# A constant product moved behind each turn of transposes, and the last weights loaded in blocks of 8, 3, 1, 1, 1

## The chip, the cores and the metric

The kernel runs on one core of a Trainium2 chip. The metric is the time of one execution on the device in microseconds (us): the median of three runs before the change. One further execution was profiled; all durations below come from it.

## The reference

One decoding step for a batch of two: attention of 32 query heads over the last 4096 positions of a cache with 8 key/value heads, and a small dense block with the Mish activation, mixed by a gate.

```python
W = min(4096, max(256, Sk // 4))                     # 4096 of 32768 positions
q = (x @ wq).reshape(B, Sq, Hq, Dh)                  # B 2, Sq 1, D 512, Hq 32, Dh 128
scores = jnp.einsum("bhqd,bhkd->bhqk", q, k) * (Dh ** -0.5)
o = jnp.einsum("bhqk,bhkd->bhqd", softmax(scores), v)
a = o.reshape(B, Sq, Hq * Dh) @ wo                   # 4096 x 512
h = jnp.einsum("bsd,df->bsf", x, w1) + b1            # 512 x 1792
b = jnp.einsum("bsf,fd->bsd", h * jnp.tanh(softplus(h)), w2)   # 1792 x 512
g = sigmoid((x * gate_w).sum(-1, keepdims=True))
return g * a + (1 - g) * b
```

Everything is float32. About 91 MB of weights and cache are read once.

## The kernel before

**Loads.** All large inputs are streamed by the sync engine's queue (SP) into two buffers of 4 MB, `buf_a` and `buf_b`, which take turns: wq in two halves, then for each of 8 key/value heads its keys into `buf_b` and its values into `buf_a`, then w1 into `buf_b`, wo in two halves (`buf_a`, then `buf_b`), and at last w2. A load waits until TensorE has finished the step that read the buffer before (L356 to L361). SP issues in the order of the program, so a load that waits holds back all that stand behind it.

**w2** is 14 blocks of 128 x 512 (256 KB each). `CUTS` (L35) gives the cuts into five loads. The first two loads go into `buf_a`, behind its first `PART` = 5 places, and wait for the step "A wo"; the other three are single blocks, go into a small tensor `rest` of their own, and wait for nothing but their turn on SP (L363 to L366).

**Steps of TensorE (PE).** A "B" step (`step_b`, L406) works through the 16 places ("slots") of `buf_b`, an "A" step (`step_a`, L417) through those of `buf_a`: one product of a 128 x 32 stationary operand with 128 x 512 for each slot. A float32 product shows as two records in the profile, so a step has 32. Slot s writes the 32-row strip s % 4 of its bank, and slots on different strips run side by side. A "T" step is a "turn" (L409): wait for the semaphore `st`, which says that another engine has written the tile `turn`; four transposes of it; and one small product with `ones` (L413) whose end is told on the semaphore `pe`, on which VectorE (DVE), ScalarE (ACT), GpSimd (POOL) and SP wait. The order of steps is the list at L128: B q0, T q0, A q1, B s0, T p0, T q1, A v0; then B s, T p, A v for each head 1 to 7 (for the last one with T mx between T p7 and A v7); then B h, T ms, T oa, T ob, T hs, A wo, B wo, A w2. PE runs this as a loop over three pieces of code: after a turn a bit of a register says whether another turn follows or an A step (L414 to L416).

**The constant product** is `idle_work` (L392): the identity matrix times itself repeated, 128 x 128 by 128 x 512, into a bank that nobody reads. It runs in the loop "spin" (five times after each A step, once after the tenth), and, before the change, once ahead of each A step.

**The last step** A w2 uses its first 5 slots with zero weights; slot `PART` waits for the first w2 load (semaphore `s4`), slot `PART + CUTS[1]` for the second (`s12`) (L419). VectorE then adds the bank to `sums` (L322). After that `finish` (L329) multiplies the three blocks in `rest` and `sums` into one bank, in the order block 11, block 12, sums, block 13; VectorE copies the result (L344), and SP stores it (L367).

Of the kernel before, what the change touches and what calls it, by code (L numbers as in the profile page):

```python
# [31 lines left out]
SMALL = DC * B + DC + FC  # L32
SCALE = DH ** -0.5
CAP = 20.0
CUTS = (0, 6, 11, 12, 13, 14)  # L35
ROWS = (24, 104)
WIDE = 2 * Q - B
PART = SLOTS - CUTS[2]
SPINS = 5
# [46 lines left out]
def decode_kernel(nc, res, stored, small, wq, k_in, v_in, w1, wo, w2, out):  # L86
    def sb(name, *shape, parts=P):
        n = 1
        for s in shape:
            n *= s  # L90
        t = nc.alloc_sbuf_tensor(name, [parts, n], F32).ap()
        if len(shape) == 1:
            return t
        names = "abcd"[: len(shape)]
        return t.rearrange(f"p ({' '.join(names)}) -> p {' '.join(names)}", **dict(zip(names[1:], shape[1:])))
# [5 lines left out]
    buf_b = sb("buf_b", CHUNK)  # L101
    rest = sb("rest", FC - CUTS[2], D)
    sm = sb("sm", SMALL)
    xT = sm[:, : DC * B].rearrange("p (c b) -> p c b", b=B)
    gw = sm[:, DC * B : DC * B + DC]
    b1 = sm[:, DC * B + DC :]
    sizes = (SLOTS * Q, SLOTS * Q, HKV * BH + B, HKV * BN * (Q + REP), (FC - CUTS[2]) * WIDE, WIDE)
    zeros = sb("zeros", sum(sizes))
# [8 lines left out]
    sa, sb_, st, s4, s12, sx = (nc.alloc_semaphore(n) for n in ("sa", "sb", "st", "s4", "s12", "sx"))  # L117
    sr = [nc.alloc_semaphore(f"sr{x}") for x in range(FC - CUTS[2])]
    pe = Lane(nc, nc.tensor, "pe")
# [180 lines left out]
    for i, (dst, sem) in enumerate(((la, sa), (lb, sb_))):  # L300
# [11 lines left out]
    t = pool.add(lambda: G.tensor_tensor(nu, nu, de, op=ALU.mult), t)  # L312
    act2_ok = pool.add(lambda: G.tensor_tensor(act2[:, :, Q - B : Q], nu[:, CUTS[2] :], ho[:, CUTS[2] :], op=ALU.mult),
                       t, ho_ok)
    sums = sb("sums", D)
    t = act.add(lambda: S.copy(sums, g_a), at("A wo"))
    pool.add(lambda: G.memset(la[:, : PART * Q], 0.0), t, sem=sa, by=got + 2)
    pool.add(lambda: G.tensor_tensor(la.rearrange("p (s q) -> p s q", q=Q)[:, PART:, ::RS], nu[:, : CUTS[2]],
                                     ho[:, : CUTS[2]], op=ALU.mult), sem=s4)
# [49 lines left out]
    def slots(bank, weights, buf, ready):  # L369
        for s in range(SLOTS):  # L370
            if s in ready:
                T.wait_ge(*ready[s]).then_inc(ready[s][0], -ready[s][1])  # L372
            ins = T.matmul(bank[Q * (s % NJ) : Q * (s % NJ) + Q, :], weights[:, s * Q : (s + 1) * Q],  # L373
                           buf[:, s * D : (s + 1) * D], start=(s < NJ), stop=(s >= SLOTS - NJ))
            if s == SLOTS - 1:
                ins.then_inc(pe.sem, 1)
# [5 lines left out]
    with nc.Block(no_gpsimd_drain=True) as block:  # L382
        @block.sync
        def _(eng):
            sp.emit(eng)

        @block.tensor
        def _(eng):
            base = nc.cur_bb
            n, again, bit, spin = (nc.alloc_register(eng.engine, x) for x in ("steps", "again", "bit", "spin"))  # L390

            def idle_work():  # L392
                T.matmul(b_idle, ident, ident[:, None, :].to_broadcast([P, NT, P]), start=True, stop=True)  # L393


            def part(name):
                nc.switch_body(name, parent=base, valid_engines=[eng.engine])

            eng.reg_mov(n, FULL - steps_a)
            eng.reg_mov(again, turns)  # L400
            eng.br("step_b")
            part("spin")
            idle_work()
            eng.reg_add(spin, spin, 1)
            eng.br_lt(spin, SPINS, "spin", "step_b")
            part("step_b")  # L406
            slots(g_b, lb, buf_b, {0: (sb_, got + 1)})
            eng.br_eq(n, FULL, "step_a", "turn")
            part("turn")  # L409
            T.wait_ge(st, 1).then_inc(st, -1)  # L410
            for c in range(NT):
                T.transpose(t_b[:, c * P : (c + 1) * P], turn[:, c * P : (c + 1) * P], ident)  # L412
            T.matmul(b_s[:, : HKV * BH + B], ones, kx, start=True, stop=True).then_inc(pe.sem, 1)  # L413
            eng.reg_alu(bit, again, 1, ALU.bitwise_and)  # L414
            eng.reg_alu(again, again, 1, ALU.logical_shift_right)
            eng.br_eq(bit, 1, "turn", "step_a")  # L416
            part("step_a")  # L417
            idle_work()
            slots(g_a, la, buf_a, {0: (sa, got + 2), PART: (s4, got + 1), PART + CUTS[1]: (s12, got)})  # L419
            eng.reg_add(n, n, 1)  # L420
            eng.reg_alu(spin, n, FULL, ALU.bitwise_and)
            eng.br_lt(n, FULL + 1, "spin", "products")
            part("products")
            pe.emit(eng)

        @block.vector
        def _(eng):
            dve.emit(eng)

        @block.scalar  # L430
        def _(eng):
            act.emit(eng)

        @block.gpsimd
        def _(eng):
            pool.emit(eng)
# [56 lines left out]
```

## Time and profile before

| | |
|---|---|
| median of three runs | 222.13 us (221.76 to 222.42) |
| the profiled execution's own time | 222.3 us |
| its span, first to last instruction | 220.3 us |
| PE busy | 157.9 us, 72% of the span |
| DVE, ACT, POOL busy | 12%, 8%, 6% |
| read from memory | 91.24 MB, 414 GB/s over the span |
| constant products (L393) | 114 records, 57 of them products |
| granted TensorE clock, mean | 0.953 |

A profiled time starts at the span's start. Between span and own time lie 2.0 us that do not show in the profile. A row of the timeline has start, duration, engine, line, operation, what it writes and reads, the count of merged records, and in brackets how long the engine was idle before it and what ended that. SPq rows are issues of transfers by SP. A row of the table of windows has for each engine its busy time and number of records, then the granted clock (1.00 is full speed), the mean busy share of the 16 transfer engines, and what they moved in GB/s.

### The profile page before, as it was taken

Reading aid. Unit: us, or ns where it says so; the run is one execution under the profiler, and the core shown is the slowest. Engines: PE = TensorE matmul, PEld = TensorE weight load, DVE = VectorE, ACT = ScalarE, POOL = GpSimd, SP = SyncE. Lnnn points to the kernel's source line nnn. Section 1 sums busy time; section 2 is a strip of 40 time slices with the busy share of each in tenths; the row PEclk is TensorE's granted clock in tenths of the full one; section 3 lists DMA queues with packets and bytes.
Section 4 is the critical chain, followed back from the end, with each engine's and each line's share of the span. In section 5 each row is a group of like instructions: output and inputs, shape, how many; then the busy total and the mean of one; then the engine's idle time right before and its main releaser. Section 6 shows DMA issues by size and latency. Waiting matters only on the chain. (4 is left out here: it accounts for less than half of the span.)

```text
span 220.3 us, 2342 instructions
## 1 busy us (share of the span) xinstructions
PE 157.9 (72%) x940; PEld 57.7 (26%) x940; DVE 26.8 (12%) x49; ACT 16.6 (8%) x39; POOL 14.2 (6%) x44
## 2 busy tenths in 40 slices
PE   0058976799587659747965974776599599859785
PEld 0012322323122223212322321222233323342222
DVE  0000001011111103010310301021020103241011
ACT  0021001200200110020011002001100210021000
POOL 4040101000100100010010001001000030003000
PEclk9999999589999999996999999999979979988999
DMA  7999999999999999999999999999999999999880
GB/s 286 406 453 411 446 422 434 458 399 470 393 470 405 452 417 440 440 416 464 393 470 405 458 417 440 428 428 452 405 464 393 470 422 440 416 440 440 332 358 23
DMA packets 3985, 91.30 MB, mean 414 GB/s; under 512 B 576, under 2 KB 656, under 8 KB 1040
## 3 DMA queue, kind: packets, MB, share of 16 engines
q1 hardware_dynamic: 3840, 91.27, 96.6%
q10 hardware_dynamic: 144, 0.01, 0.1%
q8 instruction: 1, 0.02, 0.0%
HBM read 91.24 MB, written 0.04 MB: 414 GB/s over the span
## 5 line engine op out<-in xcount | busy, mean ns | idle before, releaser
L373 PE MATMUL bank<-buf_a,zeros 128*32 128x512 f32 x352 | 47.2, 664 | 16.7 <-PEq L372 16.7
L373 PE MATMUL bank<-buf_b,zeros 128*32 128x512 f32 x352 | 42.5, 626 | 23.2 <-PEq L372 23.2
L393 PE MATMUL bank<-ident 128*128 128x512 f32 x114 | 56.9, 633 | 0.0
L393 PEld LDWEIGHTS bank<-ident 128*128 128x128 f32 x114 | 20.7, 197 | 26.4 <-issue 26.4
L373 PEld LDWEIGHTS bank<-buf_a,zeros 128*32 128x32 f32 x352 | 13.3, 120 | 51.6 <-issue 51.3
L373 PEld LDWEIGHTS bank<-buf_b,zeros 128*32 128x32 f32 x352 | 12.0, 114 | 51.7 <-issue 51.7
L412 PE MATMUL bank<-ident,turn 128*128 128x128 f32 x60 | 10.3, 298 | 20.1 <-PEq L410 20.1
L209 ACT ACTIVATE turn<-bank,mx 128x512 f32<-128x512 f32 x8 | 5.5, 687 | 132.1 <-DVE mx L207 132.1
L412 PEld LDWEIGHTS bank<-ident,turn 128*128 128x128 f32 x60 | 6.8, 149 | 29.4 <-issue 29.4
L230 DVE TENSOR_TENSOR om<-bank,pick 128x512 f32<-128x512 f32 x8 | 5.5, 692 | 73.2 <-PE bank L373 73.2
L207 DVE TENSOR_REDUCE mx<-bank 128x1 f32<-128x512 f32 x8 | 5.5, 692 | 64.7 <-PE bank L373 64.7
L202 POOL COPY zeros<-zeros 128x512 f32<-128x512 f32 x8 | 4.9, 616 | 125.9 <-PE bank L373 125.9
L233 DVE TENSOR_REDUCE od<-om 128x128 f32<-128x512 f32 x8 | 8.3, 1036 | 0.3
L413 PE MATMUL bank<-zeros,ones 128*128 128x66 f32 x30 | 5.6, 273 | 0.0
L211 ACT COPY zeros<-bank 128x512 f32<-128x512 f32 x8 | 4.7, 585 | 7.9 <-PE bank L413 7.9
L413 PEld LDWEIGHTS bank<-zeros,ones 128*128 128x128 f32 x30 | 5.2, 217 | 0.0
L182 ACT ACT_TABLE_LOAD x1 | 1.3, 1283 | 14.7 <-POOL ident L165 14.7
L158 POOL MEMSET zeros<- 128x2490 f32 x1 | 2.2, 2173 | 0.3 <-POOLq L478 0.3
L226 POOL TENSOR_TENSOR ms<-ms,top 8x64 f32<-8x64 f32 x2 | 0.6, 308 | 24.1 <-DVE top L224 24.0
L175 DVE TENSOR_REDUCE zeros<-xg 128x2 f32<-128x8 f32 x1 | 0.2, 161 | 14.0 <-POOL xg L162 14.0
L321 DVE TENSOR_TENSOR sums<-sums,bank 128x512 f32<-128x512 f32 x1 | 0.7, 686 | 9.0 <-PE bank L373 9.0
L273 ACT COPY turn<-od 128x512 f32<-128x512 f32 x1 | 0.6, 617 | 14.7 <-PE bank L413 14.7
(68 smaller groups left out, 23.6 us busy)
## 6 DMA issues: line engine op xcount, KB each, us to landing
buf_b<-in_k SPq DMA_DIRECT2D x8, 4096.0 KB, 15.5
buf_a<-in_v SPq DMA_DIRECT2D x8, 4096.0 KB, 15.5
buf_b<-in_wq SPq DMA_DIRECT2D x1, 4096.0 KB, 12.4
buf_a<-in_wq SPq DMA_DIRECT2D x1, 4096.0 KB, 21.6
buf_a<-in_wo SPq DMA_DIRECT2D x1, 4096.0 KB, 13.6
buf_b<-in_wo SPq DMA_DIRECT2D x1, 4096.0 KB, 15.2
buf_b<-in_w SPq DMA_DIRECT2D x1, 3584.0 KB, 14.3
buf_a<-in_w SPq DMA_DIRECT2D x1, 1536.0 KB, 8.6
```

The source lines that it names most:

```text
L158: zero_ok = t = pool.add(lambda: G.memset(zeros, 0.0))
L182: act.add(lambda: S.activation(turn, g_b, AF.Copy, scale=SCALE), xs_ok, id_ok, at("B q0"), sem=st)
L202: pool.add(lambda kv=kv: G.tensor_copy(lb.rearrange("p (m j q) -> p m j q", m=BN, j=NJ), qz[:, kv, : BN * Q].rearrange("p (m q) -> p m q", ...
L207: mx_ok = dve.add(lambda kv=kv: V.tensor_reduce(mx[:, kv : kv + 1], g_b, axis=AX.X, op=ALU.max, negate=True), before_b)
L209: act.add(lambda kv=kv: S.activation(turn, g_b, AF.Exp, bias=mx[:, kv : kv + 1], accum_out=ls[:, kv : kv + 1]), mx_ok, sem=st)
L211: act.add(lambda: S.copy(la, t_b), at(f"T p{kv}"), sem=sa, by=1 if kv else 2)
L230: t = dve.add(lambda: V.tensor_tensor(om, g_a.rearrange("p (m d) -> p m d", m=BN), pick[:, :, None].to_broadcast([P, BN, DH]), op=ALU.mult ...
L233: dve.add(lambda kv=kv: V.tensor_reduce(od[:, kv], om.rearrange("p m d -> p d m"), axis=AX.X, op=ALU.add), t, sem=sa)
L373: ins = T.matmul(bank[Q * (s % NJ) : Q * (s % NJ) + Q, :], weights[:, s * Q : (s + 1) * Q], buf[:, s * D : (s + 1) * D], start=(s < NJ), s ...
L393: T.matmul(b_idle, ident, ident[:, None, :].to_broadcast([P, NT, P]), start=True, stop=True)
L412: T.transpose(t_b[:, c * P : (c + 1) * P], turn[:, c * P : (c + 1) * P], ident)
L413: T.matmul(b_s[:, : HKV * BH + B], ones, kx, start=True, stop=True).then_inc(pe.sem, 1)
```

## The change

The constant product is now issued in the turn, directly behind the small product of L413, and no longer at the start of `step_a`. So every one of the 15 turns is followed by one, and no A step is preceded by one unless a turn stands ahead of it. That adds one behind each turn that is followed by another turn (T p0, T p7, T ms, T oa, T ob), and takes the one ahead of A w2 away, which has no turn ahead of it. The cuts of w2 become 8, 3, 1, 1, 1 blocks instead of 6, 5, 1, 1, 1; so slot 5 of A w2 waits for the load of 8 blocks, and slot 13 (it was slot 11) for that of 3.

```diff
-CUTS = (0, 6, 11, 12, 13, 14)
+CUTS = (0, 8, 11, 12, 13, 14)
...
             T.matmul(b_s[:, : HKV * BH + B], ones, kx, start=True, stop=True).then_inc(pe.sem, 1)
+            idle_work()
             eng.reg_alu(bit, again, 1, ALU.bitwise_and)
             eng.reg_alu(again, again, 1, ALU.logical_shift_right)
             eng.br_eq(bit, 1, "turn", "step_a")
             part("step_a")
-            idle_work()
             slots(g_a, la, buf_a, {0: (sa, got + 2), PART: (s4, got + 1), PART + CUTS[1]: (s12, got)})
```

On PE, the piece of code from the transposes of a turn to the start of an A step (`bank<-ident 128x512` is the constant product, `bank<-buf_a,zeros` the 16 slots; L414 to L417 are the register operations and the branch):

```order
 L412 MATMUL bank<-ident,turn 128x128 x4
 L413 MATMUL bank<-zeros,ones 128x66
-L414 REGISTER_ALU
+L393 MATMUL bank<-ident 128x512
 L415 REGISTER_ALU
-L416 COMPARE_AND_BRANCH
-L393 MATMUL bank<-ident 128x512
+L416 REGISTER_ALU
+L417 COMPARE_AND_BRANCH
 L373 MATMUL bank<-buf_a,zeros 32x512 x16
```

The constant product has moved from behind the branch, where only A steps pass, to ahead of it, where every turn passes.

On SP, the end of its program, from the loads of wo on (`in_w` is w2 here; 3072 columns are 6 blocks):

```order
 L350 DMA buf_a<-in_wo 128x8192
 L350 DMA buf_b<-in_wo 128x8192
-L350 DMA buf_a<-in_w 128x3072
-L350 DMA buf_a<-in_w 128x2560
+L350 DMA buf_a<-in_w 128x4096
+L350 DMA buf_a<-in_w 128x1536
 L350 DMA rest<-in_w 128x512 x3
 L367 DMA out<-res 80x128
```

The number of loads, their order and the sum of their bytes stay; only the cut between the first two moves.

## The prediction

> **What bounds the kernel now.** I read the page's slices and queues first, then a table of windows, then the timeline of the end.
>
> ```profile
> DMA  7999999999999999999999999999999999999880
> q1 hardware_dynamic: 3840, 91.27, 96.6%
> ```
>
> The transfers are busy from the first slice to the last but one: the 91.27 MB set the time, and work of PE beside a full stream costs nothing. So I looked for the places where the stream is not full. In the windows below the last two columns are share and GB/s.
>
> ```profile
> 0.74:2.74 2.00, 0.00 (x0) 0.00 (x0) 0.00 (x0) 0.00 (x0) 2.00 (x1) 1.00 0.80 229
> 2.74:3.74 1.00, 0.00 (x0) 0.00 (x0) 0.00 (x0) 0.00 (x0) 0.16 (x1) 1.00 0.47 197
> 160.00:203.00 43.00, 36.95 (x216) 14.16 (x209) 9.39 (x24) 3.45 (x9) 3.83 (x16) 0.90 1.01 434
> 204.00:206.00 2.00, 0.36 (x5) 0.19 (x8) 0.00 (x0) 0.00 (x0) 0.28 (x2) 1.00 0.69 242
> 206.00:208.00 2.00, 2.00 (x24) 0.72 (x20) 0.00 (x0) 0.00 (x0) 0.00 (x0) 1.00 0.96 369
> 208.00:214.00 6.00, 5.78 (x40) 1.47 (x32) 0.69 (x1) 0.00 (x0) 0.00 (x0) 1.00 0.97 391
> 214.00:215.00 1.00, 0.03 (x4) 0.06 (x5) 0.00 (x0) 0.00 (x0) 0.00 (x0) 1.00 0.31 121
> 215.00:217.00 2.00, 2.00 (x25) 1.11 (x26) 0.04 (x1) 0.00 (x0) 0.00 (x0) 1.00 0.10 32
> ```
>
> From 160 to 203 the stream runs at 434 GB/s, which is 27 for each of 16 engines. At 204 to 206 it falls to 242, at 206 to 208 to 369: 2 x (434 - 242) + 2 x (434 - 369) = 514 KB are missing, 1.2 us of the full stream. And it ends unevenly: the bulk is done at about 214.3 (share 0.97, then 0.31), but from 215 to 217 some 32 GB/s go on, little more than one engine's 27. One engine, hardly more, is about 2 us behind. The issues tell what happens at 204:
>
> ```profile
> 190.40 0.33 SPq L350 DMA_DIRECT2D buf_b<-in_wo  x1
> 203.14 0.80 SPq L350 DMA_DIRECT2D buf_a<-in_w  x2
> buf_b<-in_wo SPq DMA_DIRECT2D x1, 4096.0 KB, 15.2
> buf_a<-in_w SPq DMA_DIRECT2D x1, 1536.0 KB, 8.6
> buf_a<-in_w SPq DMA_DIRECT2D x1, 1280.0 KB, 11.3
> ```
>
> The second half of wo has landed at 190.40 + 15.2 = 205.6. The w2 loads are issued at 203.14, 2.5 us ahead, when "A wo" has freed `buf_a`. How long an issue takes to fill the stream is seen at the start: the first load is issued at 0.74, and until 3.74, 3.0 us later, the rate is still 197 to 229. So w2 is issued too late by half a microsecond or more, and some engines run dry. The first w2 load lands at 211.7, the second at about 203.57 + 11.3 = 214.9 (its issue is the second of the two in 0.80 us). The end hangs on that second load:
>
> ```profile
> 214.97 1.45 PE L373 MATMUL bank<-buf_a,zeros 128*32 128x512 f32 x9 [1.19 <-PEq L372]
> 216.26 0.59 PE L373 MATMUL bank<-buf_a,zeros 128*32 128x512 f32 x1
> 216.96 0.69 DVE L322 TENSOR_TENSOR sums<-sums,bank 128x512 f32<-128x512 f32 x1 [6.74 <-PE bank L373]
> 217.70 0.43 PE L334 MATMUL bank<-sums,zeros 128*32 128x128 f32 x8 [0.41 <-DVE sums L322]
> 217.94 0.40 PE L334 MATMUL bank<-rest,zeros 128*32 128x128 f32 x8
> 218.73 0.36 SPq L367 DMA_DIRECT2D out<-res  x1
> ```
>
> Load lands 214.9, five slots (10 records) until 216.85, addition until 217.65, the product with the sums and the last block, copy, store. The last single block must be there by 217.94; the windows say it lands before 217.0.
>
> **The change part by part.**
>
> *The cut 8, 3.* Behind the second load stand slots 13, 14, 15 instead of 11 to 15. Slots on different strips run side by side; 11 and 15 share one, so before, four records follow each other on it: the last starts 216.26 - 214.97 = 1.29 us after the first, 0.43 a record. After, each strip has two records, and the last starts 0.43 after the first. That is **-0.86 us** on the path. The first load grows by two blocks of 256 KB, 512 / 434 = 1.2 us later; its eight slots (four records on each strip, 1.72 us) must then fit between its landing and the second's, which are 3 blocks or 768 / 434 = 1.8 us apart. They just fit; if not, 0.1 or 0.2 us is lost, which I leave to the range. Bytes and packets' order stay, so the second load lands no later for it.
>
> *The five added products.* What matters is whether they move "A wo", whose end issues w2. The turns in front of it:
>
> ```profile
> 190.76 0.34 PE L413 MATMUL bank<-zeros,ones 128*128 128x66 f32 x2
> 192.17 0.63 PE L412 MATMUL bank<-ident,turn 128*128 128x128 f32 x4 [1.07 <-PEq L410]
> 194.19 0.63 PE L412 MATMUL bank<-ident,turn 128*128 128x128 f32 x4 [1.22 <-PEq L410]
> 195.03 0.42 DVE L264 TENSOR_REDUCE o<-bank 128x128 f32<-128x256 f32 x1 [0.98 <-PE bank L413]
> 196.16 0.98 PE L412 MATMUL bank<-ident,turn 128*128 128x128 f32 x4 [1.18 <-PEq L410]
> 197.26 2.02 PE L393 MATMUL bank<-ident 128*128 128x512 f32 x2
> 197.51 0.56 DVE L278 RECIPROCAL r<-bank 128x64 f32<-128x64 f32 x1 [1.49 <-PE bank L413]
> 198.47 0.33 DVE L301 TENSOR_TENSOR zeros<-o,r 128x32 f32<-128x32 f32 x2
> 199.21 3.86 PE L373 MATMUL bank<-buf_a,zeros 128*32 128x512 f32 x32
> 135.49 1.07 PE L393 MATMUL bank<-ident 128*128 128x512 f32 x2
> 139.19 3.64 PE L373 MATMUL bank<-buf_a,zeros 128*32 128x512 f32 x32 [2.62 <-PEq L372]
> 142.88 0.33 SPq L350 DMA_DIRECT2D buf_a<-in_v  x1
> ```
>
> Between these turns PE waits 1.07, 1.22 and 1.18 us for the engines that fill `turn`. At full clock a constant product takes 1.07 us (the row at 135.49), and its two records leave room for the next after 0.43 each, 0.86 in all. So it fits into each of the three waits, the first by 0.1 to 0.2 us: cost **0**, or, if the next transposes had to wait for its very end, 0.1 a turn, 0.3 in all. The cover is the chain of VectorE and ScalarE. At half clock it takes 2.02 us (197.26) and does not fit; then 0.8 to 1.0 a turn are lost. The products behind T p0 and T p7 stand in steps whose loads are issued long before the stream needs them, so they cost nothing, and the one ahead of A w2 that goes away stood before a wait for the first load: nothing either.
>
> *What they do to the clock.* The profile shows the clock in windows of 3.41 us:
>
> ```profile
> 117.79:121.20 3.41, 1.35 (x16) 0.56 (x20) 0.00 (x0) 0.00 (x0) 0.00 (x0) 1.00 0.98 423
> 121.20:124.62 3.42, 3.42 (x27) 1.25 (x20) 1.03 (x2) 0.00 (x0) 0.00 (x0) 1.00 0.98 422
> 172.40:175.81 3.41, 1.25 (x10) 1.17 (x11) 0.34 (x1) 1.46 (x4) 0.00 (x0) 1.00 0.91 394
> 175.81:179.23 3.42, 3.42 (x14) 1.18 (x16) 0.46 (x2) 0.56 (x2) 1.76 (x8) 0.50 1.00 431
> 192.88:196.29 3.41, 1.01 (x8) 0.84 (x8) 1.73 (x5) 1.20 (x2) 0.00 (x0) 1.00 0.94 404
> 196.29:199.71 3.42, 3.42 (x12) 1.61 (x15) 1.19 (x7) 0.23 (x1) 1.06 (x4) 0.50 0.95 412
> ```
>
> PE busy 1.25 us or less in a window is followed by one at half clock, 1.35 by full clock. The window before "T hs" has 1.01. Two constant products bring it near 3, far over the bound, so T hs and "A wo" should run at full clock. By the page "TensorE: Matmul & The Clock Gate" of the Trainium skill (Part 1: The HAM clock gate), half clock is the state after an idle window of about 3.4 us; the trace agrees on the length, but shows that 1.01 to 1.25 us of work in the window do not save it. The worth, from rows: T ob needs 195.03 - 194.19 = 0.84 us from its start to VectorE's, T hs 197.51 - 196.16 = 1.35, so VectorE starts 0.51 earlier and `la` is written (first of the two at 198.47, 0.16 long) at 198.12 rather than 198.63. "A wo" now starts at 199.21, when the slow constant product lets it; then about 0.15 behind `la`, as T oa starts 0.15 behind its tile: 198.27, **-0.94**. The step takes 142.88 - 139.19 = 3.69 from first record to issue at full clock, 203.14 - 199.21 = 3.93 now: **-0.24**. So w2 is issued 1.18 us earlier, at 201.96. The half clock at 175.81 lies in the last value step; what is won there comes on top, and I do not count it.
>
> *What the earlier issue is worth.* 201.96 + 3.0 is 204.96, before the 205.6 of wo. Bounds: nothing, if the late engine is late for a reason of its own; 2.4 us, if all engines end with the bulk (214.3 against some 216.7). I take the issue's own **-1.18**: the late engine and the landing of both large loads come earlier by as much as their issue, which lies midway.
>
> *Sum* against the profiled span: 220.3 - 0.86 - 1.18 = 218.26; with the 2.0 us outside it 220.26 against its own 222.3. The median is 0.17 lower: 222.13 - 2.04 = 220.1. With the uncounted gain before I say **220.0 us**.
>
> **The rivals.**
>
> *The stall at 204 goes altogether.* For it: 201.96 + 3.0 lies ahead of wo's landing. Against it: nothing in the trace shows when the late engine got its work. Then -0.86 - 2.4: 218.9 us.
>
> *The late engine is late by itself, or the clock still drops.* Then only the cut counts. The sums are ready at 217.70 - 0.86 = 216.84, and the last block, not after 217.0, holds the last product by 0.16 at most: -0.7 to -0.86, so 221.3 us. For the first: one engine alone trails. Against it: until 203 the share is 1.01 at 434 GB/s, with no engine behind. The page "DMA: Bandwidth & Descriptors" of the Trainium skill (Latency and other measured facts) says that engines 7 and 15 are usually slower than the others in traces; by that rule it would be 221.3, and the even stream before 203 speaks against it here.
>
> *Slower: the added products delay the turns.* Place: T oa, T ob, T hs; price: up to 0.8 to 1.0 each at half clock, some 2.4 in all, minus the 0.86 of the cut, as w2 is already issued too late and each microsecond of it reaches the end: about 223.7 us. It decides as soon as the three turns lose more than 0.86 together. For it: the first wait leaves only 0.1 to 0.2 us. Against it: half clock needs a window with 1.25 us of work or less, and with the products these windows are nearly full.
>
> **How the numbers follow.** The forecast has 0.5, the stall gone 0.2, the cut alone 0.2, slower 0.1. The range reaches from the second case to the third with their small terms: 218.7 to 221.6 us. About 0.3%, 0.67 us, is what a measurement of this kernel can tell from no change. Faster than 221.46: 0.86 (the first two cases, most of the third); same: 0.05; slower: 0.09.
>
> **What would show it.** In the profile after: the clock at 1.00 from T ms to "A wo"; the turns as far apart as before; w2 issued near 202 or earlier; the window after 204 near 434 GB/s; about 0.43 us instead of 1.29 from the first to the last start behind the second load. Wrong would be: turns further apart, w2 issued at 203 or later, or a last block that lands behind the sums and holds the last product.

## The result, and the profile after

| | before | changed |
|---|---|---|
| median of the runs | 221.94 us (4 runs, 221.17 to 222.42) | 219.71 us (4 runs, 219.43 to 219.80) |
| ratio | | 0.990, 95% interval 0.987 to 0.993 |
| profiled execution, own time | 222.3 us | 219.8 us |
| its span | 220.3 us | 217.8 us |

The change makes the kernel 2.2 us faster. The forecast was 220.0 us, 2.0 to 2.1 less than before. But the 2.5 us by which the span fell are not the sum that the forecast made.

The timeline of the changed kernel, the turns ahead of "A wo" (columns as before; the bracket is the wait before the row):

```profile
191.69 0.63 PE L412 MATMUL bank<-ident,turn 128*128 128x128 f32 x4 [0.16 <-PEq L410]
193.71 0.63 PE L412 MATMUL bank<-ident,turn 128*128 128x128 f32 x4 [0.31 <-PEq L410]
195.69 0.63 PE L412 MATMUL bank<-ident,turn 128*128 128x128 f32 x4 [0.27 <-PEq L410]
196.33 1.07 PE L393 MATMUL bank<-ident 128*128 128x512 f32 x2
197.85 3.64 PE L373 MATMUL bank<-buf_a,zeros 128*32 128x512 f32 x32 [0.45 <-PEq L372]
201.54 0.80 SPq L350 DMA_DIRECT2D buf_a<-in_w  x2
```

The waits of 1.07, 1.22 and 1.18 us have shrunk to 0.16, 0.31 and 0.27: the products lie inside them, and the turns are as far apart as before (2.02 and 1.98 us, against 2.02 and 1.97). T hs, its product and "A wo" take 0.63, 1.07 and 3.64 us, where they took 0.98, 2.02 and 3.86. w2 is issued at 201.54 instead of 203.14.

The windows of the changed kernel (last three columns: granted clock, share of the transfer engines, GB/s):

```profile
190.00:204.00 14.00, 11.36 (x66) 4.86 (x64) 4.79 (x17) 2.02 (x4) 2.46 (x10) 1.00 1.03 447
200.00:208.00 8.00, 5.01 (x37) 1.46 (x33) 0.00 (x0) 0.59 (x1) 0.55 (x3) 0.91 0.98 420
214.00:218.00 4.00, 1.39 (x36) 0.75 (x28) 0.98 (x2) 0.00 (x0) 0.00 (x0) 1.00 0.06 14
203.12:206.53 3.41, 0.99 (x12) 0.48 (x16) 0.00 (x0) 0.00 (x0) 0.00 (x0) 1.00 0.93 399
206.58:209.99 3.41, 3.41 (x23) 1.08 (x16) 0.00 (x0) 0.00 (x0) 0.00 (x0) 0.50 0.97 412
```

The same windows of the kernel before:

```profile
190.00:204.00 14.00, 10.53 (x64) 4.86 (x60) 4.78 (x17) 2.01 (x4) 2.18 (x9) 0.88 1.03 445
200.00:208.00 8.00, 6.36 (x58) 1.82 (x54) 0.33 (x1) 0.58 (x1) 1.20 (x6) 1.00 0.94 382
214.00:218.00 4.00, 2.62 (x38) 1.49 (x42) 0.69 (x1) 0.00 (x0) 0.00 (x0) 1.00 0.13 46
203.12:206.53 3.41, 1.77 (x10) 0.52 (x14) 0.00 (x0) 0.58 (x1) 0.43 (x2) 1.00 0.84 327
```

The clock is full from T ms to "A wo". From 200 to 208 the stream moves 420 GB/s instead of 382, and behind 214 next to nothing is left (14 against 46): the transfer engine that trailed is gone. The trace shows it directly. It has sixteen completion times for each load, as many as there are transfer engines. For the second w2 load they ran before from 212.20 to 214.84, the last alone and 1.1 us behind the one ahead of it; now they run from 211.52 to 212.20. The last two rows show what is new. "A wo" ends 1.6 us earlier, but wo's second half lands only 0.2 us earlier (205.4 instead of 205.6); so PE stands idle for most of 203.1 to 206.5, busy 0.99 us where it was 1.77, and the window from 206.58 on is at half clock.

The end of the changed kernel, from the transfers' table and the timeline:

```profile
buf_a<-in_w SPq DMA_DIRECT2D x1, 2048.0 KB, 8.8
buf_a<-in_w SPq DMA_DIRECT2D x1, 768.0 KB, 10.3
```

```profile
205.54 5.34 PE L373 MATMUL bank<-buf_b,zeros 128*32 128x512 f32 x32 [2.99 <-PEq L372]
210.66 3.64 PE L373 MATMUL bank<-buf_a,zeros 128*32 128x512 f32 x32
214.43 0.69 DVE L322 TENSOR_TENSOR sums<-sums,bank 128x512 f32<-128x512 f32 x1 [2.75 <-PE bank L373]
216.21 0.36 SPq L367 DMA_DIRECT2D out<-res  x1
```

The first w2 load lands at 201.54 + 8.8 = 210.3; the second is issued some 0.4 later and lands at 212.2, against 214.8 before. But "B wo" takes 5.34 us instead of 3.64, so A w2 starts only at 210.66 and runs its 16 slots in one piece of 3.64 us: it waits for neither load. The addition starts at 214.43 instead of 216.96, 2.53 us earlier, which is the change of the span. What ended last before was a load; now it is PE.

### The profile page after: what moved, and what is told of

Same layout as the page of the kernel before. It is cut to its first block, busy times and chain, and to the rows that moved or that the text cites. A ratio compares the mean times of both kernels' runs of the same rounds, so it can differ in the third digit from the quotient of the medians.

```text
span 217.8 us, 2358 instructions
## 1 busy us (share of the span) xinstructions
PE 158.2 (73%) x948; PEld 58.0 (27%) x948; DVE 26.8 (12%) x49; ACT 16.6 (8%) x39; POOL 14.2 (7%) x44
## 5 line engine op out<-in xcount | busy, mean ns | idle before, releaser
L373 PE MATMUL bank<-buf_b,zeros 128*32 128x512 f32 x352 | 44.3, 648 | 23.7 <-PEq L372 23.7
L373 PE MATMUL bank<-buf_a,zeros 128*32 128x512 f32 x352 | 46.1, 671 | 17.9 <-PEq L372 17.9
L393 PE MATMUL bank<-ident 128*128 128x512 f32 x122 | 58.3, 608 | 0.0
L393 PEld LDWEIGHTS bank<-ident 128*128 128x128 f32 x122 | 21.2, 190 | 25.6 <-issue 25.6
L373 PEld LDWEIGHTS bank<-buf_b,zeros 128*32 128x32 f32 x352 | 12.9, 117 | 53.2 <-issue 53.2
L373 PEld LDWEIGHTS bank<-buf_a,zeros 128*32 128x32 f32 x352 | 13.8, 121 | 49.2 <-issue 49.2
L412 PE MATMUL bank<-ident,turn 128*128 128x128 f32 x60 | 9.4, 280 | 15.6 <-PEq L410 15.6
L412 PEld LDWEIGHTS bank<-ident,turn 128*128 128x128 f32 x60 | 6.3, 140 | 28.3 <-issue 28.3
L413 PE MATMUL bank<-zeros,ones 128*128 128x66 f32 x30 | 5.0, 249 | 0.0
L413 PEld LDWEIGHTS bank<-zeros,ones 128*128 128x128 f32 x30 | 4.5, 191 | 0.0
```

## The experiments

Three questions. Is the cut worth anything, and where? Does the half clock in "B wo" set the new end? Is it the time of w2's issue that makes the stream lose, and not the clock? Ratios are to the kernel before, run on the same chip beside each group.

**The cut alone.** The kernel before, with

```diff
-CUTS = (0, 6, 11, 12, 13, 14)
+CUTS = (0, 8, 11, 12, 13, 14)
```

> The kernel before with the cuts 8, 3, 1, 1, 1 alone; the constant products stand where they stood. Theory of the prediction: the w2 loads are still issued at about 203.1 us and the stream still falls off at 204 to 206; the step A w2 still waits for the second load at about 214.9, and with three slots behind it instead of five the last starts 0.43 us after the first instead of 1.29: 0.86 us less, at most 0.86 and at least 0.7 with the last single block; about 221.2. Rival: the cut is worth nothing even there (the larger first load lands so late that its eight slots hold the three): within 0.2 us of the kernel before.

221.06 us (12 runs) against 221.70 (20 runs); ratio 0.9964, interval 0.9941 to 0.9988, so 0.8 us of 221.7: the theory's 0.86 lies in the interval (0.27 to 1.31 us), the rival's 0.2 does not. In the kernel before, the cut is worth something; its size is known to half a microsecond. Its profiled execution was one of its quick ones (220.1):

```profile
203.94 0.80 SPq L350 DMA_DIRECT2D buf_a<-in_w  x2
```

```profile
200.00:208.00 8.00, 7.32 (x57) 2.01 (x50) 0.22 (x1) 0.58 (x1) 0.93 (x5) 0.90 0.96 371
214.00:218.00 4.00, 1.81 (x38) 0.84 (x32) 0.98 (x2) 0.00 (x0) 0.00 (x0) 1.00 0.21 75
215.00:217.00 2.00, 0.81 (x24) 0.38 (x16) 0.72 (x2) 0.00 (x0) 0.00 (x0) 1.00 0.03 8
```

w2 is issued even later here than in the profiled execution before, at 203.94, and the stream again loses from 200 to 208 (371 GB/s). But from 215 to 217 only 8 GB/s are left, where the kernel before had 32: all transfer engines are late together here (the second load's completions run from 212.56 to 213.43), and none trails the others by 2 us.

**The products alone.** The changed kernel with the old cuts:

```diff
-CUTS = (0, 8, 11, 12, 13, 14)
+CUTS = (0, 6, 11, 12, 13, 14)
```

> The changed kernel with the old cuts 6, 5, 1, 1, 1. Theory after the result: in the changed kernel the last step of TensorE ran its 16 slots without a pause, since the step before it ran at half clock and ended after the first load had landed and so late that the second load was there before its slots; so the cut is worth nothing there and this kernel takes the changed kernel's time, 219.7, within 0.2 us. Rival, the sum of the prediction: the cut is a term of its own, and without it 0.86 us come back: 220.6.

219.84 us (9 runs), ratio 0.9914 (0.9881 to 0.9948); the changed kernel has 219.71 and 0.990 (0.987 to 0.993). The medians differ by 0.13 us, and not by the 0.86 of the prediction's sum, though the intervals alone would also hold 0.86. The trace limits it further:

```profile
210.52 3.68 PE L373 MATMUL bank<-buf_a,zeros 128*32 128x512 f32 x31
214.03 0.59 PE L373 MATMUL bank<-buf_a,zeros 128*32 128x512 f32 x1
```

The last record of "A w2" starts 3.51 us after the first. In the changed kernel, where the step runs in one piece, it is 3.64 - 0.59 = 3.05. So with the old cuts the second load still holds the step up, but by 0.46 us only. In the changed kernel the cut is worth some 0.1 us by the medians and 0.5 by this trace; the move of the products brings nearly all of the gain.

**Four products between "A wo" and "B wo".** The loop "spin" runs once there, as the register starts from 16 (`n & FULL`); shifted right by 4 it starts from 1 and runs four times. To the changed kernel:

```diff
             eng.reg_alu(spin, n, FULL, ALU.bitwise_and)
+            eng.reg_alu(spin, spin, 4, ALU.logical_shift_right)
```

> The changed kernel with four constant products instead of one between A wo and B wo. Theory: in the changed kernel TensorE now bounds the end: it waits from 202.4 to 205.5 for the second half of wo, the clock falls to half, and B wo takes 5.34 us instead of 3.64. Four products end near 205.1, just ahead of the load; B wo runs at full clock and ends near 209.2, A w2 waits for its loads again, its three last slots start behind the second load at about 212.2, and the addition starts at about 213.4 instead of 214.43: 1.0 us less, about 218.7. Rival: the transfers bound the end, and a faster B wo only waits longer: 219.7. Second rival: the four products run past the landing and B wo starts later: over 219.7.

218.98 us (6 runs, 218.69 to 219.07), ratio 0.9874 (0.9851 to 0.9897). Run again directly beside the changed kernel:

> Four products between A wo and B wo once more, now directly beside the changed kernel. Theory: the half clock in B wo costs the changed kernel 0.7 us, as the addition started 0.71 us earlier in the first run: 219.0. Rival: the first run's gain was the chip's: within 0.2 us of the changed kernel.

> The changed kernel once more, beside the next one on the same chip. Both readings expect its time again, 219.7 within 0.2 us, and a spread between its executions of under half a microsecond, since no load is issued late. If the kernel before spreads over 2 us again and this one too, the spread is not from the late issue.

218.97 us (4 runs, 218.90 to 219.25) against 219.63 (5 runs, 219.31 to 220.46): 0.66 us less, with ratios 0.9875 (0.986 to 0.9891) and 0.9897 (0.9883 to 0.9912). This version is ahead of the kernel before in both groups, and of the changed kernel in the second, where both ran. The spread of the changed kernel was not under half a microsecond: one of its five executions had 220.46. That was the profiled one; its last wo load was issued at 191.01, against 189.91 in the first profile of the changed kernel, so it had fallen back 1.1 us before the steps at issue here; why is open. It shows one thing more:

```profile
206.63 3.64 PE L373 MATMUL bank<-buf_b,zeros 128*32 128x512 f32 x32 [2.98 <-PEq L372]
```

PE waited for wo as long as in the first profile (2.98 us against 2.99), and yet "B wo" ran at full clock. The clock changes in steps of 3.41 us, and they lie elsewhere here: by its stretches at half clock one window goes from 201.56 to 204.98, with 2.09 us of work, and the next to 208.39, with 1.76, so the wait is shared between two. In the first profile 2.4 us of it lay in one window, from 203.16 to 206.57, with 1.03 us of work. So the half clock in "B wo" does not come in every execution of the changed kernel. The timeline of the first run of the four products:

```profile
205.60 3.64 PE L373 MATMUL bank<-buf_b,zeros 128*32 128x512 f32 x32 [0.42 <-PEq L372]
209.03 4.57 PE L373 MATMUL bank<-buf_a,zeros 128*32 128x512 f32 x32
213.72 0.69 DVE L322 TENSOR_TENSOR sums<-sums,bank 128x512 f32<-128x512 f32 x1 [3.66 <-PE bank L373]
```

"B wo" is back at 3.64 us, A w2 starts 1.63 us earlier, now stretches over 4.57 us because it waits for its loads again, and the addition starts at 213.72, 0.71 us before that of the changed kernel. So the half clock in "B wo" cost the changed kernel some 0.7 us, in the medians (0.66) as in these two traces; 1.0 was expected.

**The same with the old cuts.** The cuts 6, 5 in the kernel just shown.

> The same four products between A wo and B wo, with the old cuts 6, 5, 1, 1, 1. Theory: with B wo at full clock the last step waits for the second load again, so the cut has its worth again: five slots behind the landing at about 212.2, the last starts 1.29 us after the first, the addition starts at about 214.3, and the time is 0.86 us above that with the cuts 8, 3: about 219.6. Rival: the cut is worth nothing here either: the same time as with 8, 3.

219.65 us (6 runs, 219.60 to 219.77), 0.67 above the cuts 8, 3 in the same group. With "B wo" at full clock the cut has most of its worth again, 0.67 of the 0.86. The timeline shows the five slots behind the second load:

```profile
212.32 1.45 PE L373 MATMUL bank<-buf_a,zeros 128*32 128x512 f32 x9 [0.54 <-PEq L372]
213.61 0.59 PE L373 MATMUL bank<-buf_a,zeros 128*32 128x512 f32 x1
214.31 0.69 DVE L322 TENSOR_TENSOR sums<-sums,bank 128x512 f32<-128x512 f32 x1 [4.28 <-PE bank L373]
```

First to last start 1.29 us, as in the kernel before.

**Cuts 7, 4.** Again the four products, with four slots behind the second load.

> The changed kernel with four products between A wo and B wo, with the cuts 7, 4, 1, 1, 1. Theory: what counts behind the second load is how many slots share a strip, not how many there are. Slots 12 to 15 lie on four different strips, as 13 to 15 on three, so the last starts 0.43 us after the first in both: the time of the cuts 8, 3, 219.0, within 0.15 us; 6, 5, with two slots on one strip, cost 0.7. Rival: each slot behind the load costs the same: half of the way from 8, 3 to 6, 5, 219.3.

219.01 us (6 runs, 218.80 to 219.51), beside 218.98 with 8, 3 in the other group; ratios 0.9888 (0.9851 to 0.9926) and 0.9874. By the medians four slots cost what three cost:

```profile
212.95 1.06 PE L373 MATMUL bank<-buf_a,zeros 128*32 128x512 f32 x8 [0.54 <-PEq L372]
```

All eight records of the four slots are done within 1.06 us; in the two rows of the cuts 6, 5 above, the last of ten starts 1.29 after the first. The medians fit the reading that slots on one strip queue and slots on different strips do not, though the intervals would also hold the rival's 219.3.

**Two products behind each turn.** This kernel gives every turn a full clock and a late end. To the changed kernel:

```diff
             idle_work()
+            idle_work()
             eng.reg_alu(bit, again, 1, ALU.bitwise_and)
```

> The changed kernel with two constant products behind each turn. Theory: in the changed kernel the waits ahead of T oa, T ob and T hs are down to 0.16, 0.31 and 0.27 us, so a second product of 0.86 delays each by 0.55 to 0.7, and A wo, which waits 0.45, by 0.4: w2 is issued 2.2 us or a little more later, near 204, at full clock; the dip of the stream is back and the time is that of the kernel with the cuts alone, which issues at 203.94: about 221.1. Rival: the clock is what counts and the issue is early enough in any case: within 0.3 us of the changed kernel, 219.7.

221.19 us (12 runs, 220.39 to 223.63), where 221.1 was expected and the cut alone had 221.06; ratio 0.9998 (0.9966 to 1.0031). The gain of the move is gone, at full clock throughout the 14 us in question:

```profile
203.16 0.80 SPq L350 DMA_DIRECT2D buf_a<-in_w  x2
```

```profile
190.00:204.00 14.00, 14.00 (x74) 6.44 (x72) 4.79 (x17) 2.02 (x4) 2.17 (x9) 1.00 1.04 449
200.00:208.00 8.00, 6.71 (x58) 1.96 (x54) 0.33 (x1) 0.59 (x1) 1.42 (x7) 1.00 0.93 375
214.00:218.00 4.00, 2.70 (x46) 1.02 (x38) 0.98 (x2) 0.00 (x0) 0.00 (x0) 1.00 0.16 58
```

```profile
buf_a<-in_w SPq DMA_DIRECT2D x1, 768.0 KB, 10.8
```

w2 is issued at 203.16, within 0.02 us of the kernel before, and everything that marked that kernel is back: 375 GB/s from 200 to 208, transfer engines that trail behind 214 (58 GB/s), the second load at 203.56 + 10.8 = 214.4. Nothing was lost ahead of the turns: the last wo load is issued at 189.93, as in the changed kernel (189.91). So it is the time of the issue that counts; up to "A wo" the clock matters only through it. And the turns have no room for a second product, as the short waits of the changed kernel said.

**The single blocks issued first.** The kernel before, old placement and old cuts; the three blocks that wait for no step go ahead on SP:

```diff
-    for f0, f1, (dst, sem, after) in zip(CUTS, CUTS[1:], parts):
+    loads = list(zip(CUTS, CUTS[1:], parts))
+    for f0, f1, (dst, sem, after) in loads[2:] + loads[:2]:
```

> The kernel before, old placement and old cuts, with one edit: the three single blocks of w2, which wait for no step, are issued ahead of the two loads that wait for A wo. Theory: the dip of the stream at 204 to 206 is the late issue of w2. With 768 KB (1.8 us of the stream) queued behind wo from 191 us on, the stream runs on at some 430 GB/s until the two loads have come through, the dip is gone, and the second load lands at about 214.1 instead of 214.9; nothing but its five slots, the addition, the products and the store stand behind it, as before: about 0.8 us less than before, 221.0. Rival: the dip is not from the issue (a slow engine, the shape of the loads): it stays, the second load, now the last of all, lands with the last engine at about 216.7, 1.8 us later than before: about 223.5.

221.68 us (12 runs, 221.51 to 222.81) against 221.57 (23 runs, 220.58 to 223.02); ratio 1.0007 (0.9982 to 1.0032). In its time neither theory: the 0.8 us did not come, nor did the loss of 1.8. Its trace does what the theory says of the stream:

```profile
200.00:208.00 8.00, 7.02 (x58) 2.00 (x54) 0.33 (x1) 0.59 (x1) 1.43 (x7) 0.98 0.98 411
214.00:218.00 4.00, 2.96 (x42) 1.58 (x42) 0.98 (x2) 0.00 (x0) 0.00 (x0) 1.00 0.02 4
202.00:204.00 2.00, 2.00 (x17) 0.54 (x10) 0.00 (x0) 0.37 (x1) 0.00 (x0) 1.00 1.21 524
204.00:206.00 2.00, 1.02 (x6) 0.19 (x8) 0.00 (x0) 0.22 (x1) 0.43 (x2) 1.00 0.60 229
```

With loads queued behind wo, 411 GB/s from 200 to 208 and no transfer engine behind 214, although "A wo" freed its buffer no earlier (w2's two large loads are issued at 203.63). The second load lands at 214.1, as expected, and against the profiled execution before the addition starts 0.75 us earlier (216.21 instead of 216.96). But that execution is among the slower of its kind: the 23 runs beside this one have their median at 221.57, and against them nothing is won. The five-slot load is now the last of all; that this takes the rest of the saving away is argued and not shown.

The last two rows are a warning: the two-microsecond window at 204 shows 229 GB/s even here, less than the 242 from which the prediction reckoned 514 missing KB, and the one before it shows 524, above the 434 that 16 engines hold. Such short windows book packets unevenly. Over 8 us the loss before is (411 - 382) x 8 = 232 KB, or (420 - 382) x 8 = 304 KB against the changed kernel: 0.5 to 0.7 us, not 1.2. The completion times agree: half of those of the second w2 load had come by 212.47 before and by 211.93 in the changed kernel, 0.5 us earlier, but the last came at 214.84 and at 212.20. The other 2.1 us were the trailing transfer engine.

## Why the prediction was right

**Right: the place and the mechanism of the main gain.** The clock at 1.00 from T ms to "A wo", the products inside the waits of the turns, T hs and "A wo" shorter. "A wo" was forecast at 198.27 and came at 197.85, w2's issue at 201.96 and came at 201.54. The 0.42 is what the sum left uncounted: the value step ahead ran at full clock too (3.64 us instead of 4.17), and "B h" started 0.47 earlier, at 186.22 instead of 186.69.

**Too small: what the earlier issue is worth.** The prediction took "the issue's own -1.18", midway between nothing and 2.4. The second load came 2.6 us earlier, more than the upper bound. So on the loads the first rival, "the stall at 204 goes altogether", was the right one, and with PE out of the way, in the kernel with four products, its price of 218.9 us is the time (218.98). The mean loss was misread from short windows; the trailing transfer engine was read rightly. It is not late by itself, as the second rival had it: it is gone in the changed kernel and back with two products a turn. But the kernel with the cut alone, whose issue is later still, does not have it, so a late issue does not always bring it.

**Wrong for this kernel: "the cut 8, 3 ... -0.86 us on the path".** The size was right where a load ends last: 0.8 us in the kernel before, 0.67 with four products. In the changed kernel it was worth 0.1 to 0.5, as A w2 no longer waited for its loads. The step that failed is the adding: both terms were reckoned as if the second load still ended the wait. Moving the landing by 2.6 us moved the bound to PE.

**Not foreseen: half clock in "B wo".** The prediction weighed the clock up to "A wo" and stopped there. But an "A wo" that ends earlier, ahead of a load that does not come earlier, leaves PE idle longer: 0.99 us of work in the window instead of 1.77. "B wo" lost 1.70 us by it, of which about 0.7 reached the end, as the four products show; where the window falls otherwise, as in the second profile of the changed kernel, it is not lost.

So the place and the cause were right, but that the total came out within 0.3 us of the forecast is luck: a gain that was taken too small met a loss that was not seen. The loads gave 2.6 instead of 1.18. With the cut that would have made a span of 220.3 - 0.86 - 2.6 = 216.8, and the two traces with four products have 217.0 and 216.9. The half clock in "B wo" took some 0.7 of it back. The slower rival's mechanism is real, as two products a turn show by losing the gain of the move, but a single product does not trigger it.

## What to carry to other kernels

Filling waits of PE with work that nobody reads can pay on a kernel bound by transfers, if the step behind the waits frees the buffer of the last load and the work fits into the waits: one product did, two did not. When a step is made earlier, ask at once what it now waits for, and whether that new wait drops the clock of the step behind it. Terms that shorten two links of one chain may be added only while the same link ends last in both.

## What the runs showed of the hardware that was not expected

A load that is issued 1.5 to 2.5 us before the one ahead of it has landed does not cost all transfer engines alike. The completion times of the traces show how far apart they are, from the first of the sixteen to the last:

| run | w2 issued ahead of wo's landing | spread of wo's second half | spread of the second w2 load |
|---|---|---|---|
| before | 2.5 us | 0.68 us | 2.64 us |
| two products | 2.2 us | 0.39 us | 2.22 us |
| cut alone | 1.5 us | 0.52 us | 0.87 us |
| changed, first profile | 3.9 us | 0.58 us | 0.68 us |
| changed, second profile | 3.8 us | 1.41 us | 1.79 us |

In the kernel before and with two products one transfer engine, or four, fell behind after a late issue and set every later landing; with the cut alone none did, and all were late together. In the second profile of the changed kernel they were apart before w2 was issued, so a late issue is not the only way to it. Each of these is one execution. What makes a transfer engine trail stays open, and so does whether it is what spreads the kernel before from 220.58 to 223.02 us in one group of 23 runs.

The bound for half clock is not PE's busy time in a window alone. Before, 1.35 us of 3.41 kept the full clock; in the changed kernel more than that did not:

```profile
76.87:80.28 3.41, 1.43 (x8) 0.60 (x5) 0.00 (x0) 0.59 (x1) 0.00 (x0) 1.00 0.96 413
80.28:83.70 3.42, 2.79 (x16) 0.90 (x20) 0.00 (x0) 0.00 (x0) 0.00 (x0) 0.50 0.91 393
```

In the kept window the row counts 16 records, in this one 8. Their number alone does not decide, as a window with 5 records and 1.83 us of work kept the full clock (the changed kernel, from 29.08 on). In the eleven traces together, from 20 us on, every window of 3.41 us at full clock that held up to 1.32 us of PE's work was followed by half clock, and every one that held 1.65 us or more by full clock; between 1.35 and 1.6 both occur. What decides there is open.
